# Reordering the q copies, the first noisy logits and the weight conversions of a retention and two-MoE kernel, with eight unread products of zeros at the start

## The chip, the cores and the metric

The kernel runs on one core of a Trainium2 chip. A core has five engines with queues of their own: TensorE (matrix products and transposes), VectorE, ScalarE, GpSimd and SyncE. Each engine works its queue in order, waits at an instruction until the semaphores it names are there, and then goes on. Loads and stores are issued from a queue (here nearly all from SyncE's) and moved by 16 DMA engines. TensorE's weights come from the on-chip memory SBUF, its results go to PSUM banks, from which ScalarE or VectorE must copy them. The metric is the device time of the whole kernel in microseconds (us).

## The reference, cut to what matters

Three layers in a row, all in float32:

```
# 1: retention over B=2, H=8, S=768, D=64, in blocks
scores = (q_blk @ k_blk.T) * lam ** (i - j)            # lower triangle
out    = scores @ v_blk + (q_blk * lam ** (i + 1)) @ state
state  = lam ** block * state + (k_blk * lam ** (block - 1 - j)).T @ v_blk
x = out with heads side by side                         # 1536 tokens x 512

# 2: mixture of 8 experts, two for each token
noisy = x @ w_gate + log1p(exp(x @ w_noise)) * noise
best two of noisy, softmax over the two as weights
x = sum over both of weight * (relu(x @ w1[e]) @ w2[e])  # 512 -> 1024 -> 512

# 3: mixture of 8 experts, the best one, at most 384 tokens per expert
x = gate * (relu(x @ u1[e]) @ u2[e])
```

## The kernel before, in words

The work stands in three parts. The **retention** part takes 12 blocks `j` of 128 tokens (6 for each of the two batches). The **first experts** are jobs, each one expert with a number of token tiles, and so are the **second experts**. The order of instructions on each engine is fixed when the program is built: a scheduler takes them by the order in which the code names them, as soon as they look ready to its own model of time. `tc.issue_after(x)`, used through `behind(name)` with the instruction last noted in `turn[name]`, adds "not ahead of x on its engine". Nothing is reordered at run time.

For each block, with the names that the diff touches:

- `load(j + 2)` (line 145) issues the loads of k and v two blocks ahead, and in odd blocks that of q for the next pair of blocks, on SyncE's queue. `rows_of` (132) and `load_q` (138) issue one of them.
- `front_k(j)` (576) transposes k on TensorE (L580), copies it out on ScalarE (kT, L582) and scales it on GpSimd (kd, L585).
- `front_q(j)` (546), for even `j`, serves a pair of blocks. It copies q into another order of elements on ScalarE (qp, L549; for the first pair half on VectorE, L553), transposes it in two groups of four (L563), copies them out (qT, L566) and multiplies by the decay on GpSimd (qd, L571: two for each group, one for each block of the pair).
- `scores(j)` (602) makes the products q k (L609), which VectorE masks with the table `dm` (at, L613).
- `mix(j)` (637) makes the inter products of the state with qd (L643), then scores times v (L649), copied out as xT (L653); `state(j)` (615) updates the state (L623, L630, L635).
- `rows(j)` (657) turns xT into rows and gate logits (L664), copies the rows out (xr, L666), sums the logits on VectorE, and stores the rows.
- `fetch`, `convert`, `convert_low` (84 to 117) bring an expert's weights: a load of 512 KB into one of a few staging tiles, a cast to the high part on ScalarE (wh, L109), and the low part on VectorE (wl, L115), which frees the staging tile.

The loop runs `scores(j)`, `rows(j - 1)`, `front(j + 1)`, some conversions by a table of counts, `mix(j)` and one or two fetches. Into it are put the noisy logits of the first 6 blocks (`noisy`, `first_marked`, in block 7) and their ranks (`first_ranked`, `marks`, in block 8). Before the loop stand the powers of lam, which are doubled up on VectorE (L181), written to DRAM by ScalarE's queue (L183) and read back as `dm` (L186); a transpose of them (L196) gives the decays. GpSimd also makes many small constants (`more_constants`, 250), behind kd of block 1.

In the expert parts, `experts` (1046) runs each job in steps. A job with `pairs` (two of the last ones) makes its high and low products in one instruction, so that ScalarE and VectorE add the halves (hr, L901 and L902) before the split into h (L918, L919). `finish` (993) scales each tile of y, by ScalarE or VectorE in turn, and scatters it to the output from GpSimd's queue.

Of the kernel before, what the change touches and what calls it, by code (L numbers as in the profile page):

```python
# [37 lines left out]
def kernel(ctx: ExitStack, tc: tile.TileContext, q, k, v, lam, g1, gn, noise,  # L38
# [90 lines left out]
    aw = ld.enter_context(tc.tile_pool(name="aw", bufs=2))  # L129
    qkv = {}  # L130

    def rows_of(n, src, j):
        b, c = divmod(j, NC)
        t = ldp.tile([P, H, D], F32, name="ld" + n)
        nc.sync.dma_start(t, src[b, :, c * P:(c + 1) * P, :].rearrange("h p d -> p h d"))
        qkv[n, j] = t

    def load_q(j):
        b, c = divmod(j, NC)
        t = ldp.tile([P, H, 2, D], F32, name="ldq", bufs=2)  # L140
        a = q[b, :, c * P:(c + 2) * P, :].rearrange("h (p r) d -> p h (r d)", r=2)
        nc.sync.dma_start(t.rearrange("p h r d -> p h (r d)"), a)
        qkv["q", j] = t

    def load(j):
# [10 lines left out]
    rows_of("k", k, 0)  # L156
    load_q(0)
    nc.sync.dma_start(lamb, bass.AP(tensor=lam.tensor, offset=lam.offset, ap=[[0, P], [1, H]]))
    rows_of("v", v, 0)

    G = 2 * E
    gates1, gates2 = slice(0, G + P), slice(G, G + W)
# [7 lines left out]
    nc.gpsimd.tensor_copy(iw[:, 1:, G:G + P], ident[:, None, :].to_broadcast([P, DC - 1, P]))  # L170


    pw = rt.tile([P, 2, ROW], F32, name="xg", bufs=4).rearrange("p a b -> p (a b)")[:H, :2 * P]
    nc.vector.memset(pw[:, P - 1:P], 1.0)
    nc.vector.memset(pw[:, P:], 0.0)
# [2 lines left out]
    while m < P:  # L178
        n = min(m, P - 1 - m)
        a = P - 1 - m  # L180
        nc.vector.tensor_scalar(pw[:, a - n:a], pw[:, P - 1 - n:P - 1], pw[:, a:a + 1], None, op0=OP.mult)  # L181
        m *= 2
    nc.scalar.dma_start(powers.rearrange("o h m -> (o h) m"), pw)  # L183
    dm = [aw.tile([P, HP, P], F32, name=f"dm{s}", bufs=1) for s in range(2)]
    for s in range(2):
        written = nc.sync.dma_start(dm[s], bass.AP(tensor=powers.tensor, offset=powers.offset + s * 2 * P,  # L186
# [6 lines left out]
        load_q(2)  # L193
    dk = consts.tile([P, H, 1], F32, name="dk")
    ps = bank("yp3", [P, H])
    nc.tensor.transpose(ps, pw[:, :P], ident[:H, :H])  # L196
    decays = nc.vector.tensor_copy(dk[:, :, 0], ps).ins
    pq = aw.tile([P, HP, P], F32, name="pq", bufs=1)
    dec = consts.tile([P, HP, 1], F32, name="dec")
# [346 lines left out]
    def front_q(j):  # L546
        t = aw.tile([P, 2, H, D], F32, name="qp", bufs=1)
        if j:
            nc.scalar.copy(t.rearrange("p r h d -> p h r d"), qkv["q", j])  # L549
        else:  # L550
            for x, hs in ((nc.scalar.copy, slice(0, HP)), (nc.vector.tensor_copy, slice(HP, H))):
                with tc.issue_after(decays):
                    i = x(t[:, :, hs].rearrange("p r h d -> p h r d"), qkv["q", j][:, hs])  # L553
            with tc.issue_after(i.ins):
                powers_of_q()
        QT[j] = aw.tile([P, HP, 2, P], F32, name="qT")
        QD[j] = aw.tile([P, HP, 2, P], F32, name="qd")
        for g in range(2):
            ps = bank("hp", [P, 2, 2, P])
            for a in range(2):  # L560
                for r in range(2):
                    h = 2 * (2 * g + a)
                    i = nc.tensor.transpose(ps[:, a, r, :], t[:, r, h:h + 2, :].rearrange("p a d -> p (a d)"), ident)  # L563
                    turn["front"] = i.ins
            hs = slice(2 * g, 2 * g + 2)
            i = nc.scalar.copy(QT[j][:, hs].rearrange("p a c (i r) -> p a c i r", r=2)  # L566
                               .rearrange("p a c i r -> p a (c i) r"), ps.rearrange("p a r i -> p a i r"))
            turn["copied"] = i.ins
            for c in range(2):
                if j % NC or c:  # L570
                    i = nc.gpsimd.tensor_mul(QD[j][:, hs, c, :], QT[j][:, hs, c, :], pq[:, hs])  # L571
                    if "marked" in turn:
                        tc.add_manual_dep(i.ins, turn["marked"].name, mybir.DependencyInfo(
                            mybir.DependencyClass.Sync, mybir.DependencyReason.DATA), reason="behind the marks")
# [16 lines left out]
                stack.enter_context(tc.issue_after(turn[x]))  # L591
        return stack

    turn = {}

    def front(j):
        with behind("rows" if j > 1 else "state"):
            front_k(j)
            if j % 2 == 0:
                front_q(j)  # L600

# [55 lines left out]
    def rows(j):  # L657
        xr = aw.tile([P, DM], F32, name="xr")
        lt = small("lt", [P, G])
        for b in range(2):  # L660
            ps = bank(f"yp{b + 1}", [P, 2, G + P])
            with behind("scores"):
                for i in range(2):
                    tail["rows"] = nc.tensor.matmul(ps[:, i, :], XT[j][:, 2 * b + i, :], iw[:, 2 * b + i, gates1],  # L664
                                                    start=True, stop=True).ins
            nc.scalar.copy(xr[:, 2 * b * P:2 * (b + 1) * P].rearrange("p (a d) -> p a d", a=2), ps[:, :, G:])  # L666
            nc.vector.tensor_reduce(lt if b else lgs[:, j, :], ps.rearrange("p a w -> p w a")[:, :G, :], axis=AX.X, op=OP.add)
        turn["lgs"] = nc.vector.tensor_add(lgs[:, j, :], lgs[:, j, :], lt).ins
        turn["rows"] = tail["rows"]
        stored[j] = nc.sync.dma_start(x1[j * P:(j + 1) * P, :], xr).ins  # L670
# [92 lines left out]
    for j in range(NT):  # L763
        if j + 2 < NT:
            with tc.issue_after(written):
                load(j + 2)
                if j == 0:
                    nc.sync.dma_start(iw[:, :, G + P:], g2.rearrange("(c p) e -> p c e", p=P))
                    nc.sync.dma_start(nz, noise.rearrange("(t p) e -> p t e", p=P))
        if j == 2:  # L770
            with tc.issue_after(kept[1]):
                more_constants()
        scores(j)
        if j == T0 + 1:
            with behind("at"):
                noisy(s0)
                first_marked(s0)
        if j == T0 + 2:
            with behind("scores"):
                first_ranked(s0, "yp3")  # L780
                marks(ohA, cA, EARLY[0], range(T0))
        if j == TA + 1:
            with tc.high_priority(offset=300), behind("scores"):
                first_ranked(s1, "yp2")
                marks(ohA, cA, EARLY[0], range(T0, TA))
        if j:
            rows(j - 1)
        if j == TA + 1:
            with tc.high_priority(offset=300), behind("rows"):
                selA = one_hot("A", cA, aux1, *EARLY, True, "yp3", oh=ohA)  # L790
                gA = gather(selA[0], EARLY[0], EARLY[0] // EARLY[1], x1[:TA * P, :])
                turn["picked"] = selA[-1]
        if j == TA:
            with tc.high_priority(offset=400), behind("scores"):
                noisy(s1)
                turn["marked"] = first_marked(s1)
        if not j:
            mix(j)
        if j + 1 < NT:
            front(j + 1)  # L800
        with behind("copied", "lgs", "picked"):
            for _ in range({2: 1, 3: 1, 4: 2, 5: 1, 8: 1, 10: 1, NT - 1: 1}.get(j, 0)):
                convert()
                convert_low()
        if j:
            mix(j)
        if j >= 1:
            with tc.issue_after(written):
                for _ in range(2 if j == 4 else 1):
                    fetch()  # L810
    rows(NT - 1)
    ld.close()
# [25 lines left out]
    class Job:  # L838
        def __init__(self, key, size, select, source, target, first_layer, wide=False, ranked=False):
            self.key, (self.n, self.nt), self.select = key, size, select  # L840
            self.ranked = ranked
            self.rows = P if ranked else self.n // self.nt
            self.source, self.target, self.first_layer = source, target, first_layer
            self.by_token = self.nt == 1
            self.wide = wide or self.nt > 2
            self.pairs = self.wide and 2 * self.n <= 512
            self.keeps = self.quiet = False
            self.clears = 0
            self.g = self.logits = self.later = None
            self.yT = None  # L850
            self.apart = not first_layer
            self.h = {}
# [140 lines left out]
        def finish(self):  # L993
            r, n = self.rows, self.n
            for s, m in enumerate(whole_tiles(n, r)):
# [25 lines left out]
                else:  # L1021
# [3 lines left out]
                            nc.tensor.transpose(ps[:m, d * P:(d + 1) * P], self.yT[:, d, s * r:s * r + m], ident)  # L1025
                    else:
                        ps = self.y[s]
                    if s % 2:
                        nc.vector.tensor_scalar(y[:, :DM], ps[:m, :], wt, None, op0=OP.mult)
                    else:  # L1030
                        nc.scalar.activation(y[:, :DM], ps[:m, :], AF.Copy, scale=wt)
# [14 lines left out]
    def experts(jobs, last, extra=None, count=None, between=None, joins=3, sooner=()):  # L1046
# [3 lines left out]
        while j < len(jobs) and j != count:  # L1050
            job = jobs[j]
            steps = job.steps()
            for i, step in enumerate(steps):
                for _ in range(0 if job.quiet else 2 if len(steps) == 4 else 1):
                    fetch()
                step()
                nxt = jobs[j + 1] if j + 1 < len(jobs) else None
                if i == len(steps) - 1 and j + 1 < len(jobs) and j + 1 != count:
# [461 lines left out]
        body()  # L1520
    last = experts(jobs[BEFORE + 2:], last, settle)
    last.collect()
    last.finish()


# [32 lines left out]
```

## Time and profile before

| | us |
|---|---|
| median of three runs | 609.84 (609.17 to 611.41) |
| profiled execution | 611.63 |
| its span, first to last instruction | 610.0 |
| TensorE busy | 587.6 (96%) |
| VectorE busy | 373.4 (61%) |
| ScalarE busy | 280.4 (46%) |
| GpSimd busy | 182.8 (30%) |

The profile is one execution. PE is TensorE, DVE VectorE, ACT ScalarE, POOL GpSimd, SP SyncE; PEld is TensorE's weight load, which overlaps PE. `L549` is line 549 of the kernel. Times of a timeline count from the span's start. In brackets behind a row stands the idle time ahead of it and what ended it; a wait for several things is put down to the last. Retention ends at about 90 us.

### The profile page before, as it was taken

The numbers are of one execution on the slowest core, as the hardware profiler recorded it, in microseconds if no ns is written. First come the engines' busy times: TensorE is split into PE (matmuls) and PEld (weight loads), VectorE is DVE, ScalarE is ACT, GpSimd is POOL, SyncE is SP. The second block draws the span as 40 slices with busy tenths as digits, with TensorE's granted clock in tenths as the row PEclk, the third lists the DMA queues.
The fourth block names the chain that finished last, engine by engine and source line by source line (L and its number), as shares of the span: only waits on it lengthen the run. The fifth ranks groups of instructions, "written<-read, shape, count | busy, mean of one in ns | idle before, by whom it ended". The sixth has DMA issues, their size and how long they took to land. (4 is left out here: it accounts for less than half of the span.)

```text
span 610.0 us, 11507 instructions
## 1 busy us (share of the span) xinstructions
PE 587.6 (96%) x4261; PEld 555.4 (91%) x4261; DVE 373.4 (61%) x860; ACT 280.4 (46%) x488; POOL 182.8 (30%) x254
## 2 busy tenths in 40 slices
PE   5799999999999999999999999999999999999996
PEld 4698879989999999999999999998889999998995
DVE  4267769957454363464543656446887667666893
ACT  2466442146353353343533535127137467367782
POOL 3863530234205023040040410133064335231303
PEclk9799999999999999999999999999999999999999
DMA  6999921546836357457463440292189967965740
GB/s 153 207 258 248 233 91 49 173 142 199 292 95 216 107 167 243 126 179 228 123 208 123 155 140 1 61 318 83 53 267 348 353 213 235 321 219 178 258 140 34
DMA packets 106065, 110.35 MB, mean 181 GB/s; under 512 B 35879, under 2 KB 81967, under 8 KB 106000
## 3 DMA queue, kind: packets, MB, share of 16 engines
q1 hardware_dynamic: 97920, 83.57, 45.8%
q0 software_dynamic: 8064, 25.95, 12.1%
q8 instruction: 35, 0.57, 0.4%
q14 instruction: 30, 0.25, 0.1%
q10 hardware_dynamic: 16, 0.01, 0.0%
HBM read 92.48 MB, written 18.79 MB: 182 GB/s over the span
## 5 line engine op out<-in xcount | busy, mean ns | idle before, releaser
L115 DVE TENSOR_TENSOR wl<-wst,wh 128x1024 fp32r<-128x1024 f32 x107 | 133.2, 1253 | 52.4 <-ACT wh L109 50.3
L109 ACT CAST wh<-wst 128x1024 fp32r<-128x1024 f32 x107 | 111.3, 1048 | 32.9 <-PE yp L835 25.6
L834 PE MATMUL hp<-x,wh 128*128 128x372 f32 (+9 forms) x352 | 116.3, 331 | 0.8 <-ACTq L1386 0.4
L835 PE MATMUL hp<-x,wh 128*128 128x372 f32 (+9 forms) x352 | 116.3, 331 | 0.0
L836 PE MATMUL hp<-x,wl 128*128 128x372 f32 (+9 forms) x352 | 115.2, 328 | 0.0
L918 ACT ACTIVATE h<-hp 128x372 fp32r<-128x372 f32 (+9 forms) x88 | 41.3, 470 | 157.5 <-PE hp L836 147.5
L834 PE MATMUL yp<-h,wh 128*128 128x372 f32 (+8 forms) x320 | 106.3, 334 | 0.0
L836 PE MATMUL yp<-h,wl 128*128 128x372 f32 (+8 forms) x320 | 106.3, 332 | 0.0
L835 PE MATMUL yp<-h,wh 128*128 128x372 f32 (+8 forms) x320 | 105.6, 330 | 0.0
L919 DVE SCALAR_TENSOR_TENSOR h<-hp,h 128x372 fp32r<-128x372 f32 (+9 forms) x88 | 46.4, 528 | 61.3 <-ACT h L918 61.1
L1038 POOL DMA_INDIRECT x<-y,Rdst x25 | 24.7, 989 | 178.0 <-DVE y L1012 175.9
L834 PEld LDWEIGHTS hp<-x,wh 128*128 128x128 f32 x352 | 66.1, 188 | 1.8 <-ACTq L1386 0.7
L835 PEld LDWEIGHTS hp<-x,wh 128*128 128x128 f32 x352 | 66.2, 188 | 0.7 <-DVE x L1186 0.2
L836 PEld LDWEIGHTS hp<-x,wl 128*128 128x128 f32 x352 | 66.2, 188 | 0.0
L835 PEld LDWEIGHTS yp<-h,wh 128*128 128x128 f32 x320 | 60.3, 188 | 0.4 <-DVE h L919 0.4
L836 PEld LDWEIGHTS yp<-h,wl 128*128 128x128 f32 x320 | 60.3, 188 | 0.2 <-issue 0.2
L834 PEld LDWEIGHTS yp<-h,wh 128*128 128x128 f32 x320 | 60.0, 188 | 0.3 <-issue 0.2
L826 DVE TENSOR_TENSOR x<-tr,x 128x128 fp32r<-128x128 f32 (+11 forms) x68 | 27.3, 435 | 27.1 <-ACT x L825 26.5
L533 POOL TENSOR_TENSOR xg<-xg 128x512 f32<-128x512 f32 (+1 forms) x16 | 26.2, 1640 | 44.7 <-DMA xg<-x,Tsrc 29.1
L825 ACT CAST x<-tr 128x128 fp32r<-128x128 f32 (+11 forms) x68 | 24.4, 387 | 33.0 <-PE tr L824 32.6
L522 POOL DMA_INDIRECT xg<-x,Rsrc x25 | 29.0, 1159 | 18.4 <-DVE Rsrc L490 11.1
L1003 PE MATMUL tr<-iw,yT 128*128 128x136 f32 (+2 forms) x224 | 34.2, 288 | 0.1
(384 smaller groups left out, 1029.3 us busy)
## 6 DMA issues: line engine op xcount, KB each, us to landing
wst<-in_moe_w_dram SPq DMA_DIRECT2D x107, 512.0 KB, 4.9
more<-in_moe_w_dram SPq DMA_DIRECT2D x21, 512.0 KB, 4.7
ldk<-in_k_dram SPq DMA_DIRECT2D x12, 256.0 KB, 5.0
ldq<-in_q_dram SPq DMA_DIRECT2D x6, 512.0 KB, 6.8
ldv<-in_v_dram SPq DMA_DIRECT2D x12, 256.0 KB, 5.4
x<-xr SPq DMA_DIRECT2D x12, 256.0 KB, 4.2
out_dram<-zero SPq DMA_DIRECT2D x12, 256.0 KB, 5.1
dm<-powers SPq DMA_DIRECT2D x2, 256.0 KB, 3.8
```

Of the source, the lines that this page charges most:

```text
L109: tail["cast"] = nc.scalar.copy(hi, st).ins
L115: tail["low"] = nc.vector.tensor_sub(lo, st, hi.bitcast(F32)).ins
L522: i = nc.gpsimd.indirect_dma_start(out=r, out_offset=None, in_=x, in_offset=bass.IndirectOffsetOnAxis(ap=src(s)[:m], axis=0))
L533: tail["both"] = nc.gpsimd.tensor_add(a, a, b).ins
L826: v_ = nc.vector.tensor_sub(lo[:, d, :n], ps[:, :n], hi[:, d, :n].bitcast(F32))
L834: nc.tensor.matmul(ps, a[0], b[0], start=start, stop=False)
L835: nc.tensor.matmul(ps, a[0], b[1], start=False, stop=False)
L836: tail["pe"] = nc.tensor.matmul(ps, a[1], b[0], start=False, stop=stop).ins
L918: tail["act"] = nc.scalar.activation(hh, ps, AF.Relu).ins
L919: tail["dve"] = nc.vector.scalar_tensor_tensor(hl, ps, 0.0, hh.bitcast(F32), op0=OP.max, op1=OP.subtract).ins
L1003: nc.tensor.matmul(ps[:m, i, :], self.yT[:, 2 * b + i, s * r:s * r + m], iw[:, 2 * b + i, gates2], start=True, stop=True)
L1038: i = nc.gpsimd.indirect_dma_start(out=target, out_offset=bass.IndirectOffsetOnAxis(ap=dst, axis=0), in_=y, in_offset=None, bounds_check=t ...
```

## The change

- **Start.** The first v load is issued behind the last step of the powers instead of among the first loads. The first q load is split into two halves by heads. TensorE multiplies a tile of zeros by itself six times at the start, ahead of the transpose of the powers, and twice more between the first k transposes and the first q transposes; nobody reads the result.
- **q copies.** From the second pair on, the copy qp is put behind the copies xr of the block before on ScalarE.
- **Noisy logits and ranks.** They stand behind the front of the next block instead of ahead of the row products.
- **Conversions and fetches.** The conversion of block 2 moves to block 5. The eight fetches are made in blocks 1, 2, 2, 4, 4, 6, 6, 8 instead of 1, 2, 3, 4, 4, 5, 6, 7.
- **Late.** In jobs with pairs one low conversion is issued ahead of step 1. In the last job y is scaled half on VectorE and half on ScalarE.

```diff
@@ loads @@
     def rows_of(n, src, j):
-        nc.sync.dma_start(t, src[b, :, c * P:(c + 1) * P, :].rearrange("h p d -> p h d"))
+        i = nc.sync.dma_start(t, src[b, :, c * P:(c + 1) * P, :].rearrange("h p d -> p h d"))
+        return i
...
     def load_q(j):
-        nc.sync.dma_start(t.rearrange("p h r d -> p h (r d)"), a)
+        n = H if j else HP
+        for h in range(0, H, n):
+            nc.sync.dma_start(t[:, h:h + n].rearrange("p h r d -> p h (r d)"), a[:, h:h + n])
...
-    rows_of("v", v, 0)
+    def unread(n):
+        ps = bank("yp1", [P, P])
+        for _ in range(n):
+            turn["front"] = nc.tensor.matmul(ps, zero, zero, start=True, stop=True).ins
+
+    turn = {}
+    unread(6)
...
     nc.scalar.dma_start(powers.rearrange("o h m -> (o h) m"), pw)
+    wait_for(rows_of("v", v, 0), last)
...
-    nc.tensor.transpose(ps, pw[:, :P], ident[:H, :H])
+    with tc.issue_after(turn["front"]):
+        nc.tensor.transpose(ps, pw[:, :P], ident[:H, :H])
@@ front_q, front @@
-            nc.scalar.copy(t.rearrange("p r h d -> p h r d"), qkv["q", j])
+            with behind("xr"):
+                nc.scalar.copy(t.rearrange("p r h d -> p h r d"), qkv["q", j])
...
-        with behind("rows" if j > 1 else "state"):
+        with behind("rows" if j > 1 else "state" if j else "front"):
             front_k(j)
+        if not j:
+            with behind("front"):
+                unread(2)
+        with behind("rows" if j > 1 else "state" if j else "front"):
             if j % 2 == 0:
                 front_q(j)
@@ rows @@
-            nc.scalar.copy(xr[...], ps[:, :, G:])
+            i = nc.scalar.copy(xr[...], ps[:, :, G:])
+            turn["xr"] = i.ins
@@ the loop over blocks @@
         scores(j)
-        if j == T0 + 1:
-            with behind("at"):
-                noisy(s0)
-                first_marked(s0)
-        if j == T0 + 2:
-            with behind("scores"):
-                first_ranked(s0, "yp3")
-                marks(ohA, cA, EARLY[0], range(T0))
...
-            for _ in range({2: 1, 3: 1, 4: 2, 5: 1, 8: 1, 10: 1, NT - 1: 1}.get(j, 0)):
+            for _ in range({3: 1, 4: 2, 5: 2, 8: 1, 10: 1, NT - 1: 1}.get(j, 0)):
                 convert()
                 convert_low()
+        if j == T0 + 2:
+            with behind("front", "lgs"):
+                first_ranked(s0, "yp3")
+                marks(ohA, cA, EARLY[0], range(T0))
+        if j == T0 + 1:
+            with behind("at", "copied", "lgs"):
+                noisy(s0)
+                first_marked(s0)
...
-                for _ in range(2 if j == 4 else 1):
+                for _ in range({1: 1, 2: 2, 4: 2, 6: 2, 8: 1}.get(j, 0)):
                     fetch()
@@ finish @@
-                    if s % 2:
+                    if self.ends:
+                        nc.vector.tensor_scalar(y[:, :DM // 2], ps[:m, :DM // 2], wt, None, op0=OP.mult)
+                        nc.scalar.activation(y[:, DM // 2:DM], ps[:m, DM // 2:], AF.Copy, scale=wt)
+                    elif s % 2:
@@ experts @@
+                if job.pairs and i == 1:
+                    convert_low()
                 step()
@@ the last job @@
     last.collect()
+    last.ends = True
     last.finish()
```

## Rows read from the trace of the kernel before

**Rows 1.** The page, shares of the span: engine, busy us (share), instructions.
```profile
PE 587.6 (96%) x4261; PEld 555.4 (91%) x4261; DVE 373.4 (61%) x860; ACT 280.4 (46%) x488; POOL 182.8 (30%) x254
```
**Rows 2.** Waits of TensorE, 0 to 100 us: waiter <- releaser, total us, times, longest.
```profile
PE yp L196 <- DVE xg L181: 4.5, 1, 4.5
PE yp L643 <- ACT xT L653: 4.1, 1, 4.1
PE hp L563 <- ACT qp L553: 1.4, 1, 1.4
PE hp L580 <- DMA ldk<-in_k_dram: 1.4, 2, 0.8
...
PE tr L609 <- ACT kT L582: 0.3, 1, 0.3
```
**Rows 3.** Stretches A:B: length, busy us by engine, granted clock, DMA share, GB/s.
```profile
15.00:19.10 4.10, 0.00 (x0) 0.01 (x1) 0.00 (x0) 1.66 (x3) 4.10 (x45) 0.90 1.22 234
19.10:25.10 6.00, 5.98 (x32) 5.54 (x33) 1.48 (x3) 0.83 (x3) 5.27 (x42) 0.50 0.84 179
25.10:30.00 4.90, 4.83 (x66) 4.28 (x65) 1.86 (x5) 3.46 (x6) 4.08 (x6) 1.00 0.78 215
30.00:57.00 27.00, 26.59 (x336) 24.44 (x335) 18.56 (x39) 17.42 (x31) 13.84 (x14) 1.00 1.00 263
57.00:72.00 15.00, 13.50 (x166) 12.08 (x165) 12.28 (x36) 8.33 (x18) 8.00 (x9) 1.00 0.97 254
```
**Rows 4.** Timeline of ScalarE: start, us, engine line op out<-in, idle before.
```profile
17.44 1.04 ACT L549 COPY qp<-ldq 128x1024 f32<-128x1024 f32 x1 [7.65 <-DMA ldq<-in_q_dram]
18.39 0.58 ACT L653 COPY xT<-yp 128x512 f32<-128x512 f32 x1
18.87 0.59 ACT L582 COPY kT<-hp 128x512 f32<-128x512 f32 x1
```
**Rows 5.** Timeline of TensorE around blocks 1 and 2.
```profile
19.12 1.62 PE L643 MATMUL yp<-qd,st 128*128 128x128 f32 x6 [4.14 <-ACT xT L653]
...
25.37 0.60 PE L563 MATMUL hp<-iw,qp 128*128 128x128 f32 x4
25.81 0.39 PE L643 MATMUL yp<-qd,st 128*128 128x128 f32 x2
26.27 0.66 PE L563 MATMUL hp<-iw,qp 128*128 128x128 f32 x4
...
28.34 1.16 PE L609 MATMUL tr<-qT,kT 64*128 64x128 f32 x16
29.43 1.25 PE L664 MATMUL yp<-iw,xT 128*128 128x144 f32 x8
30.51 0.60 PE L580 MATMUL hp<-iw,ldk 128*128 128x128 f32 x4
30.95 1.06 PE L643 MATMUL yp<-qd,st 128*128 128x128 f32 x8
```
**Rows 6.** Timeline of GpSimd: the first constant, and what follows the last.
```profile
15.48 0.20 POOL L251 MEMSET tri<- 128x128 bf16 x1
...
24.92 1.03 POOL L585 TENSOR_TENSOR kd<-ldk,dk 128x512 f32<-128x512 f32 x1
26.78 2.79 POOL L571 TENSOR_TENSOR qd<-qT,pq 128x256 f32<-128x256 f32 x4 [0.82 <-ACT qT L566]
```
**Rows 7.** Waits of TensorE, 500 to 612 us.
```profile
PE yp L891 <- DVE h L919: 0.8, 2, 0.5
...
PE hp L892 <- DVE wl L115: 0.4, 1, 0.4
```
**Rows 8.** Timeline of VectorE in the first job with pairs.
```profile
559.08 0.33 DVE L902 TENSOR_TENSOR hr<-hr,hp 128x164 f32<-128x164 f32 x1 [1.75 <-ACT hr L901]
559.32 1.22 DVE L115 TENSOR_TENSOR wl<-wst,wh 128x1024 fp32r<-128x1024 f32 x1
```
**Rows 9.** ScalarE by form: line op xcount | busy us, mean ns | idle before.
```profile
L109 ACT CAST wh<-wst 128x1024 fp32r<-128x1024 f32 x107 | 111.3, 1048 | 32.9 <-PE yp L835 25.6 <-DMA wst<-in_moe_w_dram 6.3 <-PE hp L836 0.9
...
L666 ACT COPY xr<-yp 128x256 f32<-128x256 f32 x24 | 8.8, 372 | 20.4 <-PE yp L664 17.1 <-issue 2.5
...
L1031 ACT ACTIVATE y<-yp,Twt 128x512 f32<-128x512 f32 x3 | 2.1, 690 | 3.9 <-PE yp L836 3.6 <-ACTq L1519 0.3
```

More of the change, by code (lines that the diff above doesn't have):

```diff
@@ L130, with wait_for @@
     qkv = {}
+    def wait_for(i, other):
+        tc.add_manual_dep(i.ins, other.ins.name, mybir.DependencyInfo(
+            mybir.DependencyClass.Sync, mybir.DependencyReason.DATA), reason="a transfer behind other work")
     def rows_of(n, src, j):
@@ L180 @@
         a = P - 1 - m
-        nc.vector.tensor_scalar(pw[:, a - n:a], pw[:, P - 1 - n:P - 1], pw[:, a:a + 1], None, op0=OP.mult)
+        last = nc.vector.tensor_scalar(pw[:, a - n:a], pw[:, P - 1 - n:P - 1], pw[:, a:a + 1], None, op0=OP.mult)
         m *= 2
     nc.scalar.dma_start(powers.rearrange("o h m -> (o h) m"), pw)
+    wait_for(rows_of("v", v, 0), last)
     dm = [aw.tile([P, HP, P], F32, name=f"dm{s}", bufs=1) for s in range(2)]
@@ L592, in behind @@
         return stack
-    turn = {}
     def front(j):
-        with behind("rows" if j > 1 else "state"):
+        with behind("rows" if j > 1 else "state" if j else "front"):
             front_k(j)
+        if not j:
+            with behind("front"):
+                unread(2)
+        with behind("rows" if j > 1 else "state" if j else "front"):
             if j % 2 == 0:
@@ L665, in rows @@
                                                     start=True, stop=True).ins
-            nc.scalar.copy(xr[:, 2 * b * P:2 * (b + 1) * P].rearrange("p (a d) -> p a d", a=2), ps[:, :, G:])
+            i = nc.scalar.copy(xr[:, 2 * b * P:2 * (b + 1) * P].rearrange("p (a d) -> p a d", a=2), ps[:, :, G:])
+            turn["xr"] = i.ins
             nc.vector.tensor_reduce(lt if b else lgs[:, j, :], ps.rearrange("p a w -> p w a")[:, :G, :], axis=AX.X, op=OP.add)
@@ L846, in __init__ @@
             self.pairs = self.wide and 2 * self.n <= 512
-            self.keeps = self.quiet = False
+            self.keeps = self.quiet = self.ends = False
             self.clears = 0
```

## The prediction, on record before the result was known

> **What bounds the kernel now.** I read the shares of the page first: TensorE is busy for 587.6 of 610.0 us [rows 1], so only time in which it stands still, or runs slowly, can be won. The waits of TensorE over the first 100 us name that time. The reader is to see one large entry: 4.1 us before the products L643, released by ScalarE's copy xT L653; the other entries are the start (4.5), the first q (1.4), two late k loads (1.4 in two pieces) and a copy of kT (0.3) [rows 2]. The stretches show what follows the large one: no TensorE work from 15.0 to 19.1, and then 6.0 us of work at granted clock 0.50, the lower of its two levels (1.2 GHz), before it is 1.00 again [rows 3]. ScalarE's timeline says why: its copy qp L549 for block pair 2 sits at 17.44, after 7.65 us of waiting for the load of q, and xT and kT, whose inputs were long there, stand behind it in the queue [rows 4]. After 90 us TensorE is all but gapless, so what is won early is kept to the end, unless something else is due at a fixed time.
>
> The sum is made against the profiled execution (611.63 us, span 610.0); the median of the three runs is 609.84, 1.79 lower, and I take the same gain off it.
>
> **The q copies behind xr.** For pair 2 this takes the wait away: xT(0) is copied when its products end. L643 began at 19.12 after 4.14 us idle [rows 5], so TensorE ended the k transposes at 14.98. With xT and kT at 0.59 each [rows 4], partly beside those transposes, kT is ready at about 15.7. From there, with full-clock durations [rows 5]: scores 1.16, rows 1.25, the inter products 1.06, k transposes 0.60, four q transposes 0.60 bring TensorE to 20.4. What then follows ran from 26.27 (L563) to 31.11 (end of L580) before, 4.84 us; it would end at 25.2, 5.9 us earlier. The q copy itself is hidden there: xr ends at about 18.7, the copy of 1.04 at 19.8, just as the k transposes end.
>
> But another engine is late next. TensorE then needs qd(2) from GpSimd for the inter products that began at 30.95. GpSimd runs the constants from 15.48, then kd at 24.92 (1.03), then four qd in 2.79, 0.70 apart [rows 6]. The inter products read the first and the third. Nothing in the diff moves the constants or the load that starts them. Then kd ends at 25.95, the third qd at 28.05, and the inter products, whose second half (0.53) needs it, at 28.6 instead of 32.0. **Term: -3.4**; the bounds are 0 (a new wait of the same size) and -5.9 (GpSimd's order changes too).
>
> **The later q copies (pairs 4 to 10)** had been made a whole block early; now each stands in its own block. From the start R of the row products: they end at R+1.2, the two xr copies (0.37 each [rows 9]) at R+1.7, the q copy at R+2.7. TensorE has the k transposes (0.60) and, if the order lets it, the inter products (1.06) until R+2.8, so the first q transposes are hardly late. The second four need a buffer that the kT copy (0.59) frees at R+3.3, and they end at R+4.0, where the next products may start. Without any wait the same groups take 1.25 + 0.60 + 0.60 + 0.66 + 1.06 = 4.2 [rows 5] less 0.1 of overlap at each seam, 3.75. So 0.25 for each of four, **+1.0**. Bounds: 0, and 1.1 each if the inter products don't stand ahead. In return a q copy no longer stands before kT where TensorE lost 0.3 [rows 2]: **-0.3**.
>
> **Loads and fetches.** Two k loads are late by 1.4 in all [rows 2]. From 30 to 57 us the DMA engines' share is 1.00 at 263 GB/s [rows 3]: earlier work asks for loads 3.4 us sooner from a full resource. Two things make room. In 19.1 to 30 the share is 0.84 and 0.78, so 6.0 x 0.16 + 4.9 x 0.22 = 2.0 us stand free. And one fetch fewer (five, not six) is issued ahead of the first late k load, that of block 8 (the counts of the fetch calls in the diff): 512 KB at 263 GB/s, 2.0 us. That is 4.0 against 3.4 asked for, so the waits shrink: **-0.8**, between -1.4 (gone) and +2.6 (no room is used, the gain is mostly given back).
> The Trainium skill, page SBUF — State Buffer, section "SBUF: two separate sides", gives about 436 GB/s as the peak of the DMA side. By it the stretch would have room, both waits would go, and the sum would be 0.6 lower. The trace doesn't agree: share 1.00 at 263 GB/s in these small pieces. I go by the row.
>
> **Conversions.** The one of block 2 moves to block 5, which then has two casts (1.05 each [rows 9]) between its qT copies and xT. The first was hidden; the second puts xT, and the row products behind it, off by about half its length: **+0.5** (0 to 1.05). Block 2 had slack, so nothing comes back there.
>
> **Noisy logits, ranks and marks** keep their instructions; VectorE has room (12.28 of 15.0 us in 57 to 72 [rows 3]), and no wait of TensorE above 0.2 us there names them. 0; if the cover went, an at or state step behind them would be late, at most +0.5, and -0.3 if the row sums that they stood before come sooner.
>
> **The start.** One product of 128 columns costs what L643 does in pairs: 8 instructions in 1.06, so 0.27, and up to twice that at half clock (6 in 1.62 [rows 5]). Six are at most 3.3 us and lie in the 4.5 us before the first transpose [rows 2], as the zeros are the first thing GpSimd writes. Two more, at most 1.1, lie in the 1.4 us wait for q. The halved q load lets the first copy start earlier, the v load moves behind the powers, and the clock may rise sooner; but the decay table goes through DRAM by the same chain, the second k load is issued behind it, and GpSimd's queue above starts with that k. **0**, between -0.9 and +0.3 (the products outlast their cover).
>
> **Late jobs.** In the two jobs with pairs, TensorE waits 0.4 for wl L115 and 0.8 in two pieces for h L919 [rows 7]. The first wl conversion stands at 559.32 behind hr (559.08), though VectorE had been idle for 1.75 us [rows 8]; its own row shows no wait, so its cast was done. With one conversion ahead of the step it lies in that idle time, and the second ends 1.1 us sooner, before TensorE asks. 1.2 us of waits go, less 0.1 for each hr put back: **-1.0** (0 to -1.2).
>
> **The end.** The last y (128x512) takes 0.69; halved, ScalarE's part is like xr's 0.37 for 256 columns [rows 9], VectorE's about 0.33 x 256/164 = 0.5 (an estimate from hr [rows 8]). **-0.2** (0 to -0.3): nothing follows but the scatter.
>
> Sum: -3.4 +1.0 -0.3 -0.8 +0.5 -1.0 -0.2 = -4.2. That is 607.4 for the profiled execution and **605.6** for the median.
>
> **The rivals.**
> - *GpSimd's queue is re-ordered with the rest.* If kd and qd of pair 2 come ahead of the last constants, the first term is -5.9: 603.1. For it: kd could have run earlier than 24.92, as its k follows the q that had landed at 17.44. Against: the change touches neither.
> - *The DMA engines give it back.* The loads don't come sooner, the k waits grow by 2.6 instead of shrinking by 0.8, part of it hidden: 608.4. For it: share 1.00 for 27 us.
> - *The clock falls again at the new gap.* While TensorE waits for qd it stands still for about 1.4 and then 0.9 us. The rows show a fall after 4.1 us without work and none after 1.4. If it falls, 6.0 us of work at half speed cost 3.0: 608.6. In the skill's words (TensorE: Matmul & The Clock Gate, "HAM oscillation — how this bites in real kernels") waits between bursts of products can put the clock down each time; no number above rests on that.
> - *Slower: the q copy gets on TensorE's path in each pair.* If the order on TensorE stays as it was (first four q transposes right behind the k transposes, most inter products after them), each of five pairs waits from the end of the k transposes (R+1.65) to the end of the copy (R+2.7): 1.1 x 5 = 5.5 instead of 1.0, and the time is 610.1. It decides where the inter products stand; for it speaks the order around 26 us [rows 5] (two inter products between the q transposes, the others not ahead of them), against it that the order is planned anew with the copy late.
>
> **How the numbers follow.** The forecast has 0.45, with its own range 604.0 to 607.2; the re-ordered GpSimd 0.22; the DMA 0.15; the clock 0.06; the slower case 0.12. A measurement of this kernel can tell 0.5%, 3.0 us, so faster means below 606.8. Faster: 0.36 of the forecast, all of the second, 0.04 of the rest: 0.62. The slower case reaches past 612.9 only with other bounds at their worst: 0.06. Same: 0.32. The range 602.6 to 609.4 leaves out the best end of the second case and most of the slower one.
>
> **What would show it.** The idle before L643 of block 1 gone and a clock of 1.00 from 15 to 25 us; a new wait of TensorE for POOL qd near 25 to 28; kd(2) still at about 25; the k waits at 58 and 70 not larger; xT of block 5 behind two casts; no wait of L892 for wl and of L891 for h in the pairs jobs; two half-wide y at the end. It is wrong if the inter products that began at 30.95 come less than 2 us earlier, or if that lead is gone by 90 us.

## The result, and the profile after

The changed kernel takes 613.53 us (median of 10 runs, 612.69 to 615.47), the kernel before 610.46 (10 runs): ratio 1.0054, 95% interval [1.0040, 1.0069]. It is slower by 0.5%; 605.6, 0.7% faster, had been forecast. The profiled execution took 614.56 (span 612.9). L numbers below are those of the changed kernel (front_q L566 to L588, scores L628 and L632, mix L662 to L672, rows L683, noisy L707 to L716, mbA L725, ranks L328). TensorE is busy for longer, though only eight small products (two instructions each) were added [rows 1]:

```profile
PE 592.3 (97%) x4277; PEld 559.1 (91%) x4277; DVE 375.1 (61%) x861; ACT 279.4 (46%) x488; POOL 181.8 (30%) x254
```

Waits of TensorE from 0 to 100 us, in the columns of [rows 2]. The 4.1 for xT and the k loads are gone; the second row, for mbA, is new:

```profile
PE yp L668 <- DVE at L632: 3.2, 4, 2.0
PE yp L328 <- DVE mbA L725: 2.7, 1, 2.7
...
PE yp L683 <- ACT xT L672: 1.0, 1, 1.0
...
PE hp L580 <- ACT qp L566: 0.7, 1, 0.7
PE yp L662 <- POOL qd L588: 0.7, 1, 0.7
```

TensorE and GpSimd in blocks 1 and 2, as in [rows 5, 6]. The inter products that began at 30.95 end at 28.41, with a wait for qd, and kd still stands at 24.55 behind the constants: the early gain of 3.6 us is there, as forecast.

```profile
24.84 1.25 PE L683 MATMUL yp<-iw,xT 128*128 128x144 f32 x8
...
26.36 0.69 PE L662 MATMUL yp<-qd,st 128*128 128x128 f32 x4
27.70 0.71 PE L662 MATMUL yp<-qd,st 128*128 128x128 f32 x4 [0.65 <-POOL qd L588]
```

```profile
24.55 1.04 POOL L602 TENSOR_TENSOR kd<-ldk,dk 128x512 f32<-128x512 f32 x1
25.55 2.77 POOL L588 TENSOR_TENSOR qd<-qT,pq 128x256 f32<-128x256 f32 x4
```

The stretches, with the columns of [rows 3], say where it was lost: TensorE works 1.62 of 4 us from 62, and then 7 us at granted clock 0.51.

```profile
28.00:41.00 13.00, 12.75 (x162) 11.50 (x162) 7.14 (x15) 8.01 (x14) 9.87 (x11) 1.00 1.04 277
...
62.00:66.00 4.00, 1.62 (x14) 1.43 (x13) 3.80 (x9) 2.27 (x4) 2.25 (x3) 1.00 1.15 286
66.00:73.00 7.00, 6.63 (x62) 6.07 (x62) 4.13 (x15) 0.59 (x1) 1.94 (x2) 0.51 0.40 106
```

TensorE's timeline there. The ranks stand between the first and the second of the four inter products of block 8 (two instructions each); all that follows is queued behind their wait.

```profile
63.24 0.39 PE L662 MATMUL yp<-qd,st 128*128 128x128 f32 x2
66.37 0.19 PE L328 MATMUL yp<-mbA,tri 128*128 128x7 bf16 x1 [2.74 <-DVE mbA L725]
...
66.58 1.63 PE L662 MATMUL yp<-qd,st 128*128 128x128 f32 x6
68.14 1.98 PE L668 MATMUL yp<-at,ldv 128*64 128x128 f32 x16
69.90 1.07 PE L642 MATMUL yp<-ldv,kd 128*64 128x64 f32 x16
70.90 2.08 PE L628 MATMUL tr<-qT,kT 64*128 64x128 f32 x16
```

Who is late: ScalarE's timeline (the exponential now stands behind q copy, kT and both qT copies), then GpSimd's (the qT copies also release its qd), then VectorE's, which runs the chain of the noisy logits beside it.

```profile
56.96 1.05 ACT L566 COPY qp<-ldq 128x1024 f32<-128x1024 f32 x1
57.91 0.59 ACT L599 COPY kT<-hp 128x512 f32<-128x512 f32 x1
58.81 1.07 ACT L583 COPY qT<-hp 128x512 f32<-128x512 f32 x2 [0.31 <-PE hp L580]
59.77 0.26 ACT L707 ACTIVATE ex<-lgs 128x48 f32<-128x48 f32 x1
```

```profile
59.47 2.78 POOL L588 TENSOR_TENSOR qd<-qT,pq 128x256 f32<-128x256 f32 x4 [2.91 <-ACT qT L583]
...
63.22 1.04 POOL L654 TENSOR_TENSOR st<-st,dec 128x512 f32<-128x512 f32 x1
```

```profile
60.06 0.19 DVE L708 TENSOR_SCALAR up<-ex 128x48 f32<-128x48 f32 x1 [2.56 <-ACT ex L707]
60.28 0.67 DVE L711 SCALAR_TENSOR_TENSOR cr<-up,ex 128x48 f32<-128x48 f32 x1
...
61.70 0.62 DVE L713 TENSOR_TENSOR cr<-cr,up 128x48 f32<-128x48 f32 x1
...
63.35 0.96 DVE L715 TENSOR_TENSOR ln<-ln,nz 128x48 f32<-128x48 f32 x1
...
64.83 0.69 DVE L632 TENSOR_TENSOR at<-tr,dm 128x512 f32<-128x512 f32 x1
...
66.15 0.16 DVE L725 TENSOR_SCALAR mbA<-cA 128x6 bf16<-128x6 f32 x1
```

VectorE idles 2.56 us for ex, then takes 6.25 for the chain (60.06 to 66.31), with two st and two at steps in between; the scores that L632 scales were done at 61.8. L711, L713 and L715 end about when a GpSimd instruction ends; L716, of L715's form and with GpSimd idle, takes 0.21.

### The profile page after: what moved, and what is told of

The parts are those of the page before. It is cut to its first block, busy times and chain, and to the rows that moved or that the text cites. A ratio compares the mean times of both kernels' runs of the same rounds, so it can differ in the third digit from the quotient of the medians.

```text
span 612.9 us, 11546 instructions
## 1 busy us (share of the span) xinstructions
PE 592.3 (97%) x4277; PEld 559.1 (91%) x4277; DVE 375.1 (61%) x861; ACT 279.4 (46%) x488; POOL 181.8 (30%) x254
## 3 DMA queue, kind: packets, MB, share of 16 engines
q0 software_dynamic: 8064, 25.95, 12.1%
## 5 line engine op out<-in xcount | busy, mean ns | idle before, releaser
L109 ACT CAST wh<-wst 128x1024 fp32r<-128x1024 f32 x107 | 111.1, 1048 | 32.6 <-PE yp L855 25.6
L845 ACT CAST x<-tr 128x128 fp32r<-128x128 f32 (+11 forms) x68 | 24.4, 386 | 32.8 <-PE tr L844 32.2
L549 POOL TENSOR_TENSOR xg<-xg 128x512 f32<-128x512 f32 (+1 forms) x16 | 24.3, 1523 | 43.2 <-DMA xg<-x,Tsrc 26.9
```

Source lines behind the costliest of these rows:

```text
L109: tail["cast"] = nc.scalar.copy(hi, st).ins
L845: a = nc.scalar.copy(hi[:, d, :n], ps[:, :n])
```

## The experiments

Each time stands beside runs of the kernel before on the same chip; ratios are to it.

**1. The noisy logits, ranks and marks moved back.** Theory A: this move is the loss.
```
# the changed kernel, with
+ scores(j); if j == T0+1: behind("at"): noisy, first_marked; if j == T0+2: behind("scores"): first_ranked, marks
- the same four behind front(j + 1) and the conversions
```


> The changed kernel with only the noisy logits, first marks, ranks and marks of the first six blocks put back where they stood before (blocks 7 and 8, ahead of the row products). Theory A (VectorE's chain for the noisy logits, started 2.6 us later and stretched, holds the ranks and the masked scores of block 8; TensorE waits 2.7 us for it and its clock then falls for 6.8 us): the wait L328 on mbA is gone, the granted clock is 1.00 from 18 to 90 us, and the time is 606.5 to 608.5. Rival B (the lead of 3.6 us is eaten by the DMA engines and by ScalarE in blocks 3 to 7 whatever the noisy logits do): at most 1 us better than the changed kernel, 612 or more, with k waits at blocks 8 and 10.

608.52 against 610.69, 0.9962 [0.9949, 0.9976]: 5 us under the changed kernel. No wait for mbA is left, and no half clock from 18.4 us to the last 2 us. VectorE's timeline shows the chain finished at 61.1, L715 at 0.21:

```profile
59.32 0.21 DVE L715 TENSOR_TENSOR ln<-ln,nz 128x48 f32<-128x48 f32 x1
...
60.70 0.38 DVE L725 TENSOR_SCALAR mbA<-cA 128x6 bf16<-128x6 f32 x1
```

**2. This move alone, on the kernel before.**
```
# the kernel before, with the edit of 1 reversed
```


> The kernel before with only the noisy logits, marks and ranks moved to the new places. Theory A: slower by 4 to 7 us, 614.5 to 617.5, with the wait on mbA and the fall of the clock after it. Rival B: no change beyond 1 us.

611.56 against 610.69, 1.0010 [0.9996, 1.0024], with a wait of 0.6 for mbA and no fall of the clock behind it. Theory A's size is missed: alone the move is nearly free, so something else in the change makes it dear.

**3. The wait filled with products that nobody reads.**
```
+ if j == T0 + 2: with behind("front"): unread(10, "hp")     # ahead of the ranks
```


> The changed kernel with ten more unread products of zeros on TensorE, issued between the front of block 9 and the ranks, so that they lie in the wait for mbA. Theory A (the clock falls because TensorE stands still there): the ranks still come at about 66, but the granted clock stays at 1.00, and the time is lower by 2.5 to 3.5 us, 610 to 611. Rival C (the fall at 66 us has another cause): the clock falls as before and the time is that of the changed kernel or up to 0.5 worse.

611.97 against 610.69, 1.0022 [1.0011, 1.0034], so some 2 us under the changed kernel by the ratios (2.5 to 3.5 had been expected). The stretches show full clock where it was 0.51; the chain on VectorE is as late as it was.

```profile
62.00:66.00 4.00, 3.55 (x32) 3.35 (x30) 3.80 (x9) 2.27 (x4) 2.17 (x3) 1.00 0.96 240
66.00:73.00 7.00, 6.64 (x85) 6.15 (x86) 5.82 (x21) 2.56 (x6) 2.06 (x2) 1.00 0.59 169
```

**4. Ranks and marks a block later.**
```
- if j == T0 + 2:      # first_ranked, marks
+ if j == T0 + 3:
```


> The changed kernel with the ranks and marks of the first six blocks one block later (block 9), the noisy logits as changed. Theory A in the form that the whole VectorE queue is late: the masked scores of block 8 stand behind the same chain, so TensorE waits for them instead until about 66, and the time is lower by 0.5 to 1.5 only, unless the shorter gap spares the clock (then by 4). Rival D (only the ranks' place on TensorE is wrong): the wait goes altogether and the time falls by 5 to 6 us, to 607 to 608.5.

613.30 against 610.69, 1.0042 [1.0030, 1.0054]. The wait for mbA shrinks to 0.3; waits for the scaled scores (1.3 at the longest there) and st (1.0) stand in its place. The granted clock of this profiled execution is 1.00 from 16.2 us to the kernel's end, and the time is lost all the same. It is VectorE's whole queue that is late, not one consumer.

**5. The conversions back as well.**
```
# kernel of 1, with
- {3: 1, 4: 2, 5: 2, 8: 1, 10: 1, NT - 1: 1}
+ {2: 1, 3: 1, 4: 2, 5: 1, 8: 1, 10: 1, NT - 1: 1}
```


> The changed kernel with the noisy logits, ranks and marks at their old places (it ran in 608.5 us against 610.7 of the kernel before) and, besides, with the conversions back in their old blocks (one in block 2, one in block 5, instead of none and two). Theory B, two casts in block 5 stand ahead of the copy that xT needs and hold the scaling of block 6: the wait of 1.0 us of the row products on xT and that of 0.8 us on the scaled scores of block 6 go, so 1.5 to 1.9 us less, 606.6 to 607.1 us. Rival, the cast that comes back to block 2 costs as much as the one taken from block 5, since block 2 has no more room: no change, 608.2 to 608.8 us.

608.26 against 610.73, 0.9955 [0.9939, 0.9971]: by time not told apart from 1. In the trace one cast of 1.06 us stands ahead of xT where two stood (47.40, 2.00 us), and its wait of 1.0 is gone, but this profiled execution has a half-clock stretch at 28.8 to 32.2 that that of 1 has not. Undecided here; 9 takes it up.

**6. Without the eight unread products.**
```
# kernel of 1, with
- unread(6)
- if not j: with behind("front"): unread(2)
```


> The changed kernel with the noisy logits, ranks and marks at their old places, without the eight unread products of zeros. Theory C, the products only move the half-clock stretch from before 11.4 us to 11.4 to 18.3 us, and GpSimd's multiplication of q in block 2, which ends at 28.4 us whatever comes before, takes up what they give: the half clock comes back between 18 and 25 us, TensorE reaches that point at most 0.6 us later, and the time is 608.2 to 609.1 us. Rival, the half clock then falls on the row products of the first blocks and they are late past 28 us: 1.0 to 2.0 us more, 609.5 to 610.5 us. Second rival, the products cost time ahead of the first transposes: 0.5 us less, 608.0 us.

608.70 against 610.73, 0.9963 [0.9949, 0.9977], the same as 1. The wait of 4.5 us at the start is back as a wait and costs nothing. The half clock did not come back at 18 to 25 in the profiled execution (12.3 to 15.8 only), so the reason that I had written for "no change" is not shown; that the products are worth nothing measurable is.

**7. GpSimd's 49 small fills moved out of the way.**
```
# kernel of 1, with
- past_sizes(past1, FIRST, 4); past_sizes(past2, SECOND, 3)        # in more_constants
+ if j == 5: with tc.issue_after(kept[max(kept)]): the same two
```


> The changed kernel with the noisy logits, ranks and marks at their old places, and GpSimd's 49 small fills of the table of sizes (3.9 us, 16.7 to 20.9) moved behind the multiplication of k in block 6, where GpSimd stands idle for 5.4 us. Theory, these fills hold the multiplication of q in block 2: it starts up to 2 us earlier, the wait of 0.6 us on it goes, and the wait for the q copy of 0.7 us stands next: 0.4 to 0.8 us less, 607.7 to 608.1 us. Rival G, the whole early gain was held there and comes free: 2 us less, 606.5 us. Rival H, the fills stretch VectorE's work in blocks 6 and 7 by more than they give: 0.5 us more, 609 us.

607.18 against 610.73, 0.9942 [0.9922, 0.9963]. The wait for qd is gone, and GpSimd's timeline has qd(2) at 22.51 instead of 25.6:

```profile
20.57 1.03 POOL L600 TENSOR_TENSOR kd<-ldk,dk 128x512 f32<-128x512 f32 x1
22.51 2.78 POOL L586 TENSOR_TENSOR qd<-qT,pq 128x256 f32<-128x256 f32 x4 [0.90 <-ACT qT L581]
```

The prediction's cap on its first term was this queue. The intervals of 1 and 7 overlap, so the size is not settled.

**8. Only the pairs jobs and the end.**
```
# the kernel before, with
+ if job.pairs and i == 1: convert_low()
+ last.ends = True            # the last scaling in two halves
```


> The kernel before with only the last part of the change: a low conversion ahead of each job in pairs from its second step, and the halved last scaling. By the prediction's term for the late jobs and for the end: 1.0 + 0.2 us less, 609.2 to 609.6 us beside 610.7 of the kernel before. Rival, the waits on VectorE in these jobs turn into others: no change, 610.4 to 610.9 us.

609.26 against 610.73, 0.9978 [0.9965, 0.9992]: 1.3 us, as its terms said (-1.0 and -0.2). The waits of TensorE for h and wl [rows 7] are gone, as they are in the whole change.

**9. 1, 5 and 7 together.**
```
# kernel of 1, with the edits of 5 and 7
```


> The changed kernel with the noisy logits, ranks, marks and conversions back at their old places and GpSimd's 49 small fills behind the multiplication of k in block 6. Without the conversions back it ran in 607.2 us against 610.7 of the kernel before, with waits of 1.0 us on xT (block 5) and of 1.2 us on the scaled scores. Theory B, the two casts of block 5 are the cause of the first: it goes, 1.0 to 1.5 us less, 605.7 to 606.3 us, ratio to the kernel before 0.9918 to 0.993. Rival, what the first gives, a later wait takes (on k, or on the scaled scores): no change, 606.9 to 607.5 us.

606.26 against 610.15, 0.9931 [0.9914, 0.9947]: the best of all, ahead of both kernels. Over 7 it has 0.001, which the intervals don't resolve. A wait for xT of 0.9 is still there, in block 2 now: the cast that came back there stands ahead of xT and waits itself for its weights.

```profile
28.57 1.04 ACT L109 CAST wh<-wst 128x1024 fp32r<-128x1024 f32 x1 [2.07 <-DMA wst<-in_moe_w_dram]
29.52 0.58 ACT L670 COPY xT<-yp 128x512 f32<-128x512 f32 x1
```

**10. Only the q copies behind xr.**
```
# the kernel before, with
+ turn["xr"] = i.ins            # the xr copy
+ with behind("xr"):            # around nc.scalar.copy of qp, j > 0
```


> The kernel before with one part of the change alone: each q copy behind the copies of the row products. The prediction's terms for it: 3.4 us of lead in block 2, later copies +1.0 or -0.3, so 606.5 to 608.4 us beside 610.7 of the kernel before. Theory J, the lead is there at block 2 (scores and row products 2.5 to 4 us earlier) and is eaten by a wait that stands later and that the change's other parts don't move: the loads of k (1.4 us of waits in the kernel before) or the scaled scores; 1 us or less is left, 609.4 to 610.2 us.

609.71 against 610.15, 0.9994 [0.9981, 1.0007]: not to be told from nothing. The lead is there: the row products of blocks 0 and 1 start at 17.24 and 23.55 (before 22.68 and 29.43). Then it goes: blocks 2, 4 and 6 lead by 3.1, 1.7 and 0.6 us (1.5 to 1.9 from block 7 on, where the profile of the kernel before has its two late k loads; the medians are 0.4 apart). Blocks 2 to 5, which ran almost without waits, now wait for GpSimd and VectorE. The waits of TensorE, 0 to 58 us:

```profile
PE yp L644 <- POOL qd L572: 2.1, 3, 1.2
PE yp L650 <- DVE at L614: 1.7, 4, 0.8
PE hp L564 <- ACT qp L554: 1.2, 1, 1.2
PE yp L644 <- DVE st L631: 1.0, 2, 0.8
```

**11. Only the conversions back.** Theory A against rival B (the second cast of block 5 makes the chain late).
```
# the changed kernel, with the edit of 5
```


> The changed kernel with only the conversions back in their old blocks; the noisy logits and ranks stay at their new places. Theory A, the chain of the noisy logits on VectorE behind the copies of block 7 is late by itself: the ranks still wait over 2 us, the clock may fall to half behind it, 612 to 613.5 us. Rival B, the second cast in block 5 made block 6 and with it the chain late: the wait is under 1 us, the clock holds, 609 to 610 us.

612.16 against 610.15, 1.0034 [1.0018, 1.0051]: rival B falls, the wait stays. This profiled execution has no fall of the clock behind it (its half-clock stretch lies at 27.9 to 31.3), which prices the fall: TensorE's timeline behind the same wait.

```profile
66.75 0.18 PE L328 MATMUL yp<-mbA,tri 128*128 128x7 bf16 x1 [2.75 <-DVE mbA L725]
...
66.94 0.91 PE L662 MATMUL yp<-qd,st 128*128 128x128 f32 x6
67.78 1.09 PE L668 MATMUL yp<-at,ldv 128*64 128x128 f32 x16
68.71 0.64 PE L642 MATMUL yp<-ldv,kd 128*64 128x64 f32 x16
69.27 1.16 PE L628 MATMUL tr<-qT,kT 64*128 64x128 f32 x16
```

These four groups take 3.80 here and 6.76 in the changed kernel: the fall costs 3.0 us in that execution. The wait costs another 3.0: the score products of block 9 begin 8.27 us behind those of block 8 here (61.00 and 69.27), 5.27 in experiment 1.

**12. The q order and the noisy logits, together.**
```
# the kernel before, with the edits of 2 and 10
```


> The kernel before with two parts of the change: each q copy behind the copies of the row products, and the noisy logits, ranks and marks at their new places (which alone cost 0.9 us, 611.6). Theory I, the earlier blocks take away the time that hid the chain (the wait for k in block 7): the ranks wait 2 us or more, the clock falls to half behind it, 612 to 614.5 us. Rival, the two parts add up: 0.9 us more than the kernel with the q order alone, with a wait on the ranks under 1 us, 609.5 to 611 us.

614.75 against 610.15, 1.0070 [1.0052, 1.0087]. Alone the two parts are 0.9994 and 1.0010; together they cost 4 us more than their sum. The rival of adding up falls. The wait and the stretch behind it:

```profile
PE yp L312 <- DVE mbA L707: 3.2, 1, 3.2
```

```profile
64.00:69.00 5.00, 1.76 (x21) 1.52 (x18) 4.76 (x14) 2.00 (x4) 2.04 (x2) 1.00 0.93 227
69.00:73.00 4.00, 4.00 (x48) 3.81 (x48) 2.90 (x8) 0.59 (x1) 0.04 (x1) 0.57 0.03 6
```

**13. One word less.**
```
- with behind("at", "copied", "lgs"):
+ with behind("at", "lgs"):            # noisy, first_marked
```


> The changed kernel with one word less: the noisy logits stay at their new place in the text, but are set behind the scaling of the scores and the logits only, not behind the q and k copies of the block. Theory K, that one condition is the cause: with it ScalarE's exponential starts at 59.8 us behind the two qT copies, and VectorE's chain then runs beside GpSimd's multiplication of q, which the same copies release; without it the exponential and the logarithm stand ahead of these copies, the chain ends before the scores of block 8, the wait of 2.7 us on the ranks and the half clock behind it go: 608.3 to 609.3 us beside 610.5 of the kernel before, as with all of it moved back (608.5). Rival L, the later place in the text (behind the conversions and the q and k copies of the next block) keeps the chain late anyway: 611.5 to 613.5 us, with a wait of 2 us or more.

609.31 against 610.75, 0.9974 [0.9963, 0.9986]. Theory K holds: that one condition takes away the gain. ScalarE's timeline has the exponential 5.6 us, and the logarithm just, ahead of the qT copies; no wait for mbA is left. Three steps of the chain (L715, L716, L723) still take 0.63 to 0.65 beside GpSimd, but mbA is there at 64.2 and TensorE is ready for the ranks at 65.1.

```profile
55.12 0.24 ACT L707 ACTIVATE ex<-lgs 128x48 f32<-128x48 f32 x1 [1.07 <-DVE lgs L688]
...
60.29 0.25 ACT L709 ACTIVATE ln<-up 128x48 f32<-128x48 f32 x1
60.71 1.07 ACT L583 COPY qT<-hp 128x512 f32<-128x512 f32 x2 [0.17 <-PE hp L580]
```

**14. Experiment 9 without the unread products.**
```
# kernel of 9, with the edit of 6
```


> The kernel with noisy logits, ranks, marks and conversions back and GpSimd's 49 small fills later (606.26 us against 610.15, ratio 0.9931), without the eight unread products of zeros. With the q order alone and no such products, the granted clock had risen at 12.0 us and not fallen again, and the first row products began at 17.24, against 17.8 to 18.7 with them. Theory M, the products bring a half-clock stretch at 11.4 to 18.3 us that GpSimd's queue hid as long as it was the cap; with the cap gone their removal gives 0.5 to 1.3 us: 604.9 to 605.8 us beside 610.15, ratio 0.9914 to 0.9928. Rival, another engine takes the lead up (the q copy, xT behind the cast in block 2, the scaled scores): no change, ratio 0.9928 to 0.9942. Second rival, the half clock comes back on the row products of the first blocks: ratio 0.9945 or more.

606.80 against 610.90, 0.9937 [0.9922, 0.9952], not to be told from 9: theory M's gain is missed, the first rival (another engine takes the lead up) stands. Half of theory M is in the traces: without the products the granted clock is 1.00 from 8.2 us to the last 2 us (in 9: 0.50 from 13.0 to 16.4), and the first row products start at 16.43 (17.82). A k load that is 0.9 us late at 18.6 takes part of the lead, and in block 2 the start is the same again, 29.98 and 30.15, since xT stands behind the cast; the wait there is

```profile
PE yp L676 <- ACT xT L665: 1.6, 1, 1.6
```

against 0.9 in 9.

## Why the prediction was wrong

**The step that failed** is the term for the noisy logits, ranks and marks: "VectorE has room", 0, "at most +0.5". I read VectorE's busy share and the lack of waits, and did not follow the chain from its new release to the ranks. "Copied" is the qT copies, and at j = T0 + 1 these are the copies of the next block: with them ScalarE's exponential comes at 59.77, and VectorE's chain runs beside the GpSimd work that the same copies release. Experiment 13 shows that this condition is the cause. Experiment 12 against 2 and 10 shows that it becomes dear with the q order. My account of why (the kernel before still waited 0.78 us for a k load at 58.2, and its later blocks gave the chain more time) does not hold. The trace of experiment 2 has no wait for a k load, and TensorE is ready for the ranks at the same time as in 12 (64.77 and 64.80). What differs is the chain on VectorE, in 2 and then in 12:

```profile
60.70 0.52 DVE L688 TENSOR_SCALAR up<-ex 128x48 f32<-128x48 f32 x1 [1.78 <-ACT ex L687]
...
64.63 0.72 DVE L705 TENSOR_SCALAR mbA<-cA 128x6 bf16<-128x6 f32 x1
```

```profile
61.23 0.19 DVE L690 TENSOR_SCALAR up<-ex 128x48 f32<-128x48 f32 x1 [2.56 <-ACT ex L689]
...
67.82 0.17 DVE L707 TENSOR_SCALAR mbA<-cA 128x6 bf16<-128x6 f32 x1
```

In 2 ScalarE copies q a block earlier, the qT copies and the exponential come half a us sooner, and the chain takes 4.65 us with no at step in it. In 12 it takes 6.76: two at steps (0.69 and 0.68) stand ahead of mbA, and the steps that multiply by the noise and add the logits take 1.00 and 0.97 beside GpSimd's st and kd, against 0.21 and 0.19 in 2. How much each of these does was not isolated. The Trainium skill, page SBUF — State Buffer, section "Who interferes with whom", says that a VectorE instruction with two SBUF inputs contends with a GpSimd instruction that reads SBUF, the later one waiting out the first; L715's 0.96 against 0.21 agrees.

**The size**: a wait of 2.74 and 3.0 of half clock, 5.7 us on the profiled execution; experiment 1 gets back 5.0 by medians. That these are close does not show that the clock is in the medians: the other nine runs of the changed kernel have a mean granted clock of 0.991 to 0.997, against 0.988 in the profiled one, too high for both of its half-clock stretches at full length. Filling the wait (experiment 3) gave back some 2 us; experiment 4 lost nearly as much as the change (1.0042) without a second fall in its profiled execution. So the late chain is the cause that is shown, and the share of the clock in the median stays open.

The clock was rival 3's mechanism, "the clock falls again at the new gap", at a gap that I had not seen. At the gap it named the clock held in the changed kernel (0.65 at 27.70). But in the profiled executions of experiments 5, 11, 12 and 13 it was 0.50 for 3.4 us from there (from 27.9 to 28.8), around waits for qd of 1.1 to 1.6 and then 0.65; in those of 4 and 10, with waits of 1.06 and 1.23, it was not. From the score products of block 2 to those of block 3 that is 8.93 us in 11 against 7.32 in 4, so 1.6 for the fall and not 3.0. My ground against this rival, "none after 1.4", has no row under it: the clock of the kernel before is on record only from 11.5 us, and its wait of 1.4 ends at 7.2.

**The first term** (-3.4 in block 2) was right in place and size, 3.6, and so was GpSimd's cap on it. What failed with it is the sentence that "what is won early is kept to the end": experiment 10 keeps 0.6 us of it by block 6, and where the three terms for the q copies add up to -2.7, it measures -0.4. I had asked what is late next once, in block 2, and not block by block. The term for the later q copies (+1.0) has the right sign; its mechanism, q transposes late in each pair, was not what took the lead.

**Loads**: the k waits are gone (-1.4, the better bound), but they are gone as well in the profiles of experiments 2 and 8, which leave the loads and the q copies as they were, and 14 has one of 0.9; that the change took them away is not shown. The full resource of that term was a misreading of the share (last section). **Conversions**: forecast +0.5; two casts do hold xT by a wait of 1.0, but experiments 5, 9 and 11 don't resolve a time. **The start**: 0 held for the products (experiments 6 and 14); the halved q load and the moved v load were not tested alone. **Late jobs and end**: forecast -1.2, measured -1.3 (experiment 8).

The parts add up: 1.0070 (experiment 12) times 0.9978 (8) is 1.0048; the whole change is 1.0054.

## What to carry to other kernels

When a short chain that a later product needs is moved, follow it from its new release to that product, engine queue by engine queue; the busy share of its engine says nothing about that. A condition that ties it to an instruction which also starts another engine's work puts the two side by side. And a lead won early lasts only as far as the next engine that had no waits because TensorE was late: try two parts together before calling either free.

## What the runs showed of the hardware

- A wait of TensorE of 2.74 us was followed by 6.8 us at half clock (66.0 to 72.9), and one of 2.75 by none in the profiled execution of experiment 11; one of 3.24 by 3.4 us of it in 12 (69.2 to 72.6). Two shorter waits in a row (1.06 and 0.65) were followed by 3.4 us of it in 5 and by none in 4. Waits of these lengths went either way.
- Products of zeros brought the first record of clock 1.00 to 4.6 us in the changed kernel, against 11.5 before; over all kernels it stands at 4.2 to 9.6 with them and at 8.2 to 12.1 without. But 0.50 then followed from 11.4 to 18.3, and in seven of the nine profiled executions with them there was such a fall, within 11.4 to 18.4 us. Of the four without them and with the new q order, 10, 12 and 14 had no such fall, 6 had one (12.3 to 15.8). An early rise was no gain here.
- A DMA share of 1.00 is no ceiling: 277 GB/s came at 1.04 (28 to 41 us) and 286 at 1.15 (62 to 66), against the 263 at 1.00 that I had taken for a full resource. [rows 3] had a share of 1.22 already, at 234 GB/s.
